# A state-space scan over even tokens only, with the decay scaled on ScalarE

## The chip, the cores and the metric

The kernel runs on one core of one Trainium2 chip. The metric is the device time of one execution in microseconds, as a median of several runs. Engines are named as in the profile: PE is TensorE (PEld its weight loads), DVE is VectorE, ACT is ScalarE, POOL is GpSimd, SP is SyncE, which issues DMAs.

## The reference

Two token mixers work on the same `x` of 2048 tokens by 1024 channels and are blended by a gate per token:

```python
g = sigmoid((x * gate_w).sum(-1, keepdims=True))
a = irfft2(rfft2(x) * (w_r + 1j * w_i))           # spectral branch
Lam_bar = exp(exp(log_dt) * Lam)                  # 1024 complex decays
Bu = einsum("bld,pd->blp", x, ((Lam_bar - 1) / Lam)[:, None] * Bmat)
for t in range(L):                                # state-space branch
    h = Lam_bar * h + Bu[:, t, :]
y = 2 * einsum("blp,dp->bld", hseq, Cmat).real + x * Dskip
out = g * a + (1 - g) * y
```

`x` is `A_x` in both branches. Inputs and the output are bf16.

## The kernel before

The tokens are cut into 8 chunks of 256 (`TC`), the 1024 states into 8 blocks `jb` of 128, one state per partition. Tile `h` of a chunk holds `[128, 2 (real, imaginary), 8 (jb), 256 (token)]` in bf16. A chunk goes through these steps:

- `unit_mm` (PE, L398): B times x, four psu tiles per chunk, each 32 matmuls of 256 columns. `unit_out` (ACT, L408) copies each to `h` and puts the tokens in order.
- `recur` (DVE): the complex decay is split into a radius r and a turn. `cross` (L347) and `along` (L350) multiply by a table `tab` of cosines and sines, `join_re` and `join_im` (L353, L356) add, so that what remains is a real recurrence with factor r. `carry_in` (L359) adds the last chunk's end to the first token, `scan` (L363) runs over all tokens of the block, once for the real and once for the imaginary part (`rz` holds r, and 0 at the first token of each jb, so one instruction covers many jb). `carry_part` and `carry_sum` (L368, L371) make the next carry. `cross(3)`, `along(2)`, `out_re` and `out_im` (L374, L378) turn back and multiply by the input factor. The products' scratch tile is `su` for chunks 0 and 1, and a part of `xQ` that PE has finished with for later ones.
- `c_half` and `c_part` (PE, L713 and L727): the 16 token tiles `tb` of 128 tokens, C times h, 16 matmuls per half of 512 columns. The first ten tiles go early through DRAM (`early_mm`, scaled by `scale_y`, L744), 10 to 12 (`DIAG`, with the skip term as extra matmuls, L719) and 13 to 15 (`rest`, tiles ps_q) are done last. Both tiles of chunk 7 are in `rest`; `last_out` (L899) and a store end the kernel.

Chunks 0 and 1 (`NSEP`) go through `recur` in two halves of 4 jb, later chunks in one unit. `h` has three buffers.

The spectral branch runs between these: `turn`, `fold`, `fd`, `s1` (forward transform, up to about 80 us), `s2`, `times_w`, `is1`, `is2` with evictions on ACT (L603, L637, L671), and at the end `spectral_mm` (PE, L806 and L810, tiles ps_id), `spectral_out` (ACT, L817) and the sums of `spectral` (DVE, L825 to L846). All PSUM tiles share four slots, whose turn is written out in `SLOTS`.

The order of the instructions on every engine is written out by hand: `ORDER` is a string of letters, each of which takes the next step of one of the generators, and `v` takes the next entry of `PIECES`, an index into the list `work` that `recur` fills. Each engine runs its own instructions in that order, waiting on semaphores.

Of the kernel before, what the change touches and what calls it, by code (L numbers as in the profile page):

```python
# [40 lines left out]
CARRY_POOL = ()  # L41
# [9 lines left out]
)  # L51
SLOTS = (
    "0123012310231023102310230123012031201312031203101230132031231031201312303312013213021021013010320130",
    "1220123203201320130130120321023120320321021023120312301230231201302303120",
# [3 lines left out]
    "xxxTVUVVVaTfVVrrUGTGG|Tfaaa|UafFffftafftUftxFEfTETUFffU22xSEkSTSTArxAfffUAUFTTEUfffUFbxwxbxbbTUEFbfE",  # L58
    "1bT~SSUfuFSFAUUUU2bbtbfAF1AtbbtrFttrbEffE11EbEh11SStbttfttttAg1~HtfufhA~tetFSSFrKHrtu1EAvfAEhtttvttt",
    "SSFtbbvvvAtEttH1Avthtftv1cttwv1tcthccctttvtcch~HFtvftHvvhuHtvfStEettStAHhtAeKrvFctcvvFhEEHKtvwtcSvtS",  # L60
    "hvvKc1vcc1vAAKKvv1c1v1hcvswcsLMvvveHHekMYsssnNHvvhHnsvvvJWWMvs3vsvNvvsssssnvssnvvs4NMvv4Njvhv553vhvv",
    "YvyJJL46H4vv5WWvhh5vvvMM78Jj7HHmn3nHvv8M44m6MnN77WW5jv+Yy5vvv3M845+mNY8nMJJMyvvv+467hvHMh5vN7N34vHmh",
    "4J8m+6n3h8v77HmH+55v4n64JMvNnMYy5vW83n+v7N474vJ568vYmmNJ7dh7NWj+v58v5vyvvd88MhvHHm8+MJm6h+n378vv7Hh8",
    "J+d4Y4YX5vv5NnJH6XXv7ny7mNNm8+hn8hvqivvvvvJvqyHihYivvyiqhivqqiYvNImvni+qJJmHIIiini+HinvdIIH+vvIIIqIN",
    "IiiiNmI+vvIInvvImvyJqii%NJINIJYJYmhvvv+vvvlylzvhHmplpzZZH+mZZZhlZvhPPRR++zyRRRlQDQHzRZZmRHZ+ZRZvoOZD",
    "QvlpDzzPovOvQBvZZlpPYvZZvBZDZRDRRRvzQDoloOBzoQOopZOoPOBlzlZRoDDZZvBZZRpQvzCvYZZvZZBZZPRDoQoo9RQQ9yRR",
    "0RRyCooD099C9Y990DD0D0Y00",
# [75 lines left out]
def kernel(  # L143
# [19 lines left out]
    out2 = out[0]  # L163
# [53 lines left out]
    nc.gpsimd.iota(tau_i, pattern=[[1, TC]], base=0, channel_multiplier=0)  # L217
# [5 lines left out]
    tab = tabp.tile([P, 4, 8, TC], BF16, name="tab")  # L223
# [42 lines left out]
    def radii():  # L266
        for jb in range(8):
            nc.gpsimd.tensor_copy(out=rz[:, jb, :], in_=r_sb[:, jb:jb + 1].to_broadcast([P, TC]))
            nc.gpsimd.memset(rz[:, jb, 0:1], 0.0)
            yield  # L270

    def make_tab(jp):
# [14 lines left out]
        cast(2 * jp)(out=tab[:, 1, js, :], in_=sn_f)  # L287
        yield
        t1 = tmp.tile(sh, FP32, name="t1")
        t2 = tmp.tile(sh, FP32, name="t2")  # L290
        for j in range(2):
            nc.scalar.activation(out=t1[:, j], in_=sn_f[:, j], func=ACT.Copy, scale=ci[:, 2 * jp + j:2 * jp + j + 1])
        yield
        cast(2 * jp + 1)(out=tab[:, 0, js, :], in_=cs_f)
# [5 lines left out]
        for j in range(2):  # L300
            jb = 2 * jp + j
            nc.vector.scalar_tensor_tensor(out=tab[:, 2, jb, :], in0=cs_f[:, j], scalar=cr[:, jb:jb + 1], in1=t1[:, j],
                                           op0=ALU.mult, op1=ALU.subtract)
            yield
        for j in range(2):
            jb = 2 * jp + j
            nc.vector.scalar_tensor_tensor(out=tab[:, 3, jb, :], in0=sn_f[:, j], scalar=cr[:, jb:jb + 1], in1=t2[:, j],
                                           op0=ALU.mult, op1=ALU.add)
            yield

    rz = tabp.tile([P, 8, TC], FP32, name="rz")
    carry = cpool.tile([P, 2, 8], FP32, name="carry")
# [16 lines left out]
    def small_ops():  # L329
        return nc.gpsimd if next(smalls_made) in CARRY_POOL else nc.vector  # L330

    smalls_made = itertools.count()

    def recur(c, js, home):
        n = js.stop - js.start
        on_in, on_part, on_sum = (small_ops() for _ in range(3))
        sh = [P, 2, n, TC]
        u = hs[c][:, :, js, :]

        def bc(i):  # L340
            return tab[:, i:i + 1, js, :].to_broadcast(sh)

        tmps = {}

        def cross(i):
            tmps["s"] = home()
            nc.vector.tensor_mul(out=tmps["s"], in0=u[:, ::-1], in1=bc(i))  # L347
# [7 lines left out]
        def join_im():  # L355
            nc.vector.tensor_sub(out=u[:, 1], in0=tmps["s"][:, 1], in1=u[:, 1])  # L356

        def carry_in():
            on_in.tensor_add(out=u[:, :, :, 0], in0=u[:, :, :, 0], in1=carry[:, :, js])  # L359

        def scan(ri, j, m):
            seg = u[:, ri, j:j + m].rearrange("p j t -> p (j t)")
            nc.vector.tensor_tensor_scan(out=seg, data0=rz[:, js.start + j:js.start + j + m].rearrange("p j t -> p (j t)"),  # L363
                                         data1=seg, initial=0.0, op0=ALU.mult, op1=ALU.add)

        def carry_part():
            gl = u[:, :, :, TC - 1]
            on_part.tensor_mul(out=ck[:, :, :, js], in0=gl.unsqueeze(1).to_broadcast([P, 2, 2, n]), in1=rot[:, :, :, js])  # L368

        def carry_sum():  # L370
            on_sum.tensor_add(out=carry[:, :, js], in0=ck[:, :, 0, js], in1=ck[:, :, 1, js])  # L371

        def out_re():
            nc.vector.tensor_add(out=u[:, 0], in0=u[:, 0], in1=tmps["s"][:, 0])  # L374
            done[c] = done.get(c, 0) + n

        def out_im():
            nc.vector.tensor_sub(out=u[:, 1], in0=u[:, 1], in1=tmps["s"][:, 1])  # L378
# [23 lines left out]
    def unit_out():  # L402
        for c in range(NCH):
            for q in range(2):
                for ri in range(2):
                    if (q, ri) == (0, 0):
                        hs[c] = halloc()
                    nc.scalar.copy(out=hs[c][:, ri, 4 * q:4 * q + 4].rearrange("p b (q j) -> p b q j", j=32),  # L408
                                   in_=psus.pop((c, q, ri)).rearrange("p b (j q) -> p b q j", j=32))
                    if ri == 1 and c < NSEP:  # L410
                        recur(c, slice(4 * q, 4 * q + 4), lambda: up.tile([P, 2, 4, TC], BF16, name="su"))
                    elif ri == 1 and q == 1:
                        recur(c, slice(0, 8), lambda c=c: xQ[:, 2 * (c % 2):2 * (c % 2) + 2])
# [802 lines left out]
```

## Time and profile before

| | |
|---|---|
| time, median of 3 runs | 304.7 us (304.66 to 305.07) |
| profiled execution, span from the first to the last instruction | 303.6 us |
| mean granted TensorE clock | 0.999 |
| PE, DVE, ACT, POOL busy | 296.4, 289.3, 188.5, 73.3 us |
| HBM read, written | 27.46, 23.08 MB |

The profiled execution's own time as a run is not listed apart from these; its span stands 1.1 us under the median. A row of the grouped lines has the line, the engine, the operation, out<-in, shapes and count, then busy us and the mean ns of one, then the idle us just before them with what ended it. A row of the timeline has start and length in us. Busy time of a group counts overlapping instructions once, so it is less than count times mean.

### The profile page before, as it was taken

The page shows a single profiled execution, that of the slowest core. Times are in us where ns is not written, and L with a number is a line of the kernel's source. Part 1 is how long each engine was busy: PE and PEld are TensorE (multiplying, and loading weights), DVE is VectorE, ACT ScalarE, POOL GpSimd, SP SyncE. Part 2 cuts the span into 40 slices and gives each one's busy share as a digit, 9 for nine tenths or more (in the row PEclk, how much of TensorE's full clock was granted, in tenths as well). Part 3 has the DMA queues.
Part 4 walks back from the last instruction along what each step waited for, and adds up shares of the span by engine and source line. Part 5 has one row for each costly group of instructions (what it writes and reads, how often), then busy time and mean ns, then how long its engine had stood idle before and what let it go on. Part 6 is the DMA issues. An engine that isn't in the chain of part 4 may idle for free. (4 is left out here: it accounts for less than half of the span.)

```text
span 303.6 us, 6402 instructions
## 1 busy us (share of the span) xinstructions
PE 296.4 (98%) x2568; PEld 197.4 (65%) x2592; DVE 289.3 (95%) x340; ACT 188.5 (62%) x255; POOL 73.3 (24%) x99
## 2 busy tenths in 40 slices
PE   8999999999999999999999999999999999999995
PEld 5664677878864685458553866669657986645543
DVE  2999999999999999999999999999899999999995
ACT  4999999896532383667665865529668774343400
POOL 2100420745893001110210220202011253252330
PEclk9999999999999999999999999999999999999999
DMA  6999999989999599895948798687758876978976
GB/s 208 341 201 194 253 193 310 162 142 154 268 214 241 160 259 219 181 250 189 212 96 258 163 223 225 139 294 147 242 174 185 165 88 135 160 132 143 165 153 181
DMA packets 74157, 59.35 MB, mean 196 GB/s; under 512 B 44904, under 2 KB 61680, under 8 KB 74128
## 3 DMA queue, kind: packets, MB, share of 16 engines
q1 hardware_dynamic: 66560, 49.82, 65.8%
q0 software_dynamic: 6912, 8.69, 23.0%
q10 hardware_dynamic: 656, 0.44, 0.5%
q8 instruction: 20, 0.33, 0.4%
q14 instruction: 9, 0.07, 0.1%
HBM read 27.46 MB, written 23.08 MB: 166 GB/s over the span
## 5 line engine op out<-in xcount | busy, mean ns | idle before, releaser
L398 PE MATMUL psu<-xQ,BT 128*128 128x256 bf16 x1024 | 116.5, 273 | 0.2 <-DVE X L449 0.2
L398 PEld LDWEIGHTS <-BT 128*128 128x128 bf16 x1024 | 99.0, 98 | 17.3 <-issue 4.6
L713 PE MATMUL ps_y<-CT,h 128*128 128x512 bf16 x397 | 92.5, 379 | 0.9
L363 DVE TENSOR_TENSOR_SCAN h<-rz,h 128x2048 bf16<-128x2048 f32 (+1 forms) x20 | 70.8, 3561 | 0.0
L713 PEld LDWEIGHTS <-h 128*128 128x128 bf16 x416 | 39.6, 98 | 46.3 <-issue 2.9
L785 POOL DMA_DIRECT2D y_scratch<-su x20 | 17.3, 902 | 135.7 <-ACT su L779 105.4
L408 ACT CAST h<-psu 128x1024 bf16<-128x1024 f32 x32 | 32.3, 1011 | 18.7 <-PE psu L398 13.1
L350 DVE TENSOR_TENSOR h<-h,tab 128x4096 bf16<-128x4096 bf16 (+1 forms) x20 | 37.1, 1859 | 0.1
L744 ACT ACTIVATE ye<-ps_y,omg 128x512 f32<-128x512 f32 x26 | 17.9, 689 | 26.3 <-PE ps_y L713 11.8
L347 DVE TENSOR_TENSOR xQ<-h,tab 128x4096 bf16<-128x4096 bf16 x12 | 27.4, 2284 | 1.0 <-ACT h L408 1.0
L603 ACT CAST X<-ps_s 128x1024 bf16<-128x1024 f32 x16 | 16.2, 1010 | 14.6 <-PE ps_s L594 11.2
L727 PE MATMUL ps_q<-CT,h 128*128 128x512 bf16 (+2 forms) x110 | 21.3, 348 | 0.2
L817 ACT ACTIVATE BT<-ps_id,gB 128x1024 bf16<-128x1024 f32 x14 | 15.3, 1114 | 9.9 <-PE ps_id L810 5.7
L671 ACT CAST ZT<-ps_is 128x1024 bf16<-128x1024 f32 x16 | 15.8, 1017 | 6.2 <-PE ps_is L661 6.2
L637 ACT CAST C<-ps_is 128x1024 bf16<-128x1024 f32 x16 | 15.7, 1011 | 5.1 <-DMA xQ<-in_A_x_dram 3.4
L851 POOL DMA_DIRECT2D BT<-y_scratch x10 | 13.1, 1452 | 19.7 <-DVE BT L846 13.3
L727 PEld LDWEIGHTS <-h 128*128 128x128 bf16 x112 | 10.3, 98 | 10.4 <-DVE h L378 0.5
L779 ACT ACTIVATE su<-xs,omg 128x512 f32<-128x512 bf16 x20 | 14.2, 723 | 4.1 <-DMA y_scratch<-su 2.2
L929 ACT COPY xQ<-pt 128x1024 bf16<-128x1024 bf16 x12 | 12.2, 1082 | 1.3 <-PE pt L919 1.3
L449 ACT CAST X<-ps_fd 128x1024 bf16<-128x1024 f32 x12 | 12.3, 1062 | 1.0 <-PE ps_fd L439 0.9
L617 DVE TENSOR_TENSOR UV<-X,Wb 128x2048 bf16<-128x2048 bf16 x8 | 9.6, 1220 | 0.6 <-ACT ye L744 0.6
L617 DVE TENSOR_TENSOR UV<-X,raw 128x2048 bf16<-128x2048 bf16 x8 | 9.8, 1223 | 0.2 <-ACT X L604 0.2
(200 smaller groups left out, 397.3 us busy)
## 6 DMA issues: line engine op xcount, KB each, us to landing
y_scratch<-ye SPq DMA_DIRECT2D x20, 256.0 KB, 4.6
y_scratch<-su POOLq DMA_DIRECT2D x20, 256.0 KB, 4.7
Bb<-turn_scratch SPq DMA_DIRECT2D x16, 256.0 KB, 5.2
turn_scratch<-C SPq DMA_DIRECT2D x16, 256.0 KB, 4.1
raw<-turn_scratch SPq DMA_DIRECT2D x8, 512.0 KB, 4.3
xs<-in_A_x_dram SPq DMA_DIRECT2D x13, 256.0 KB, 3.9
out_dram<-BT SPq DMA_DIRECT2D x11, 256.0 KB, 4.3
CT<-in_A_x_dram SPq DMA_DIRECT2D x5, 512.0 KB, 6.1
```

Of the source, the lines that this page charges most:

```text
L347: nc.vector.tensor_mul(out=tmps["s"], in0=u[:, ::-1], in1=bc(i))
L350: nc.vector.tensor_mul(out=u, in0=u, in1=bc(i))
L363: nc.vector.tensor_tensor_scan(out=seg, data0=rz[:, js.start + j:js.start + j + m].rearrange("p j t -> p (j t)"), data1=seg, initial=0.0, ...
L398: nc.tensor.matmul(psu[:, j, :], lhsT=BT[4 * q + j][:, ri, d8, :], rhs=xQ[:, c, d8, :], start=(d8 == 0), stop=(d8 == 7))
L408: nc.scalar.copy(out=hs[c][:, ri, 4 * q:4 * q + 4].rearrange("p b (q j) -> p b q j", j=32), in_=psus.pop((c, q, ri)).rearrange("p b (j q) ...
L603: nc.scalar.copy(out=X2, in_=ps2s[g][b])
L617: nc.vector.tensor_mul(out=UV, in0=X2s.pop((g, b)).unsqueeze(1).to_broadcast([P, 2, 2, K]), in1=fft["Wb"][g // 2 % 2][:, :, at:at + 1, :]. ...
L671: nc.scalar.copy(out=ZT[:, 4 * kp:4 * kp + 4, :, 4 * G:4 * G + 4].rearrange("p (c r) n g -> p c r n g", c=2), in_=pszs.pop((G, kp)).rearra ...
L713: nc.tensor.matmul(psy, lhsT=hs[c][:, ri, jb, P * tq:P * (tq + 1)], rhs=CT[ri][:, jb, 512 * dh:512 * (dh + 1)], start=(i == 0), stop=(i == ...
L727: nc.tensor.matmul(psq, lhsT=hs[c][:, ri, jb, P * tq:P * (tq + 1)], rhs=CT[ri][:, jb, at:at + n], start=(i == 0), stop=(i == 15))
L744: nc.scalar.activation(out=ye, in_=psys[tb][:, K * hf:K * (hf + 1)], func=ACT.Copy, scale=omg[:, tb:tb + 1])
L785: nc.gpsimd.dma_start(out=y_dram[tb, hf], in_=xgs[tb, hf], accum_op=ALU.add)
```

## The change

The recurrence is taken two tokens at a time. With even tokens e and odd tokens o, g(e) = r² g(e-2) + (u(e) + r u(e-1)) and g(o) = r g(o-1) + u(o). In place of `scan` over 256 tokens, a unit now does: `late` on ACT, the odd inputs times r, moved by one; `carry_in` into the first column of that tile; `fold_in` on DVE, an add over the even tokens; `scan` over 128 even tokens with r² (`r2_sb`, the new `rz`), real and imaginary part in one instruction for a whole chunk; `next_` on ACT, the even results times r; and `fill_in` on DVE, an add over the odd tokens. `late` and `next_` take two jb per entry of `PIECES`, so a chunk has 8 activations of each. `carry_sum` goes, its add is now in `carry_in`.

```diff
-        return pool.tile([P, 2, 8, TC], BF16, name="h")
+        return pool.tile([P, 2, 2, 8, TS], BF16, name="h")
...
+        def late(j):
+            for i in range(j, j + 2):
+                nc.scalar.activation(out=tmps["s"][:, 0, :, i, 1:TS], in_=u[:, 1, :, i, 0:TS - 1], func=ACT.Copy,
+                                     scale=r_sb[:, js.start + i:js.start + i + 1])
+
+        def carry_in():
+            first = tmps["s"][:, 0, :, :, 0]
+            if c:
+                nc.vector.tensor_add(out=first, in0=ck[:, :, 0, js], in1=ck[:, :, 1, js])
+            else:
+                nc.vector.memset(first, 0.0)
+
+        def fold_in():
             nc.vector.tensor_add(out=u[:, 0], in0=u[:, 0], in1=tmps["s"][:, 0])
...
+        def scan():
+            flat = lambda t, i: t[:, i, js].rearrange("p j t -> p (j t)") if n < 8 else t.rearrange("p r j t -> p (r j t)")
+            for i in range(2 if n < 8 else 1):
+                seg = flat(hs[c][:, 0], i)
+                nc.vector.tensor_tensor_scan(out=seg, data0=flat(rz, i), data1=seg, initial=0.0, op0=ALU.mult, op1=ALU.add)
+
+        def next_(j):
+            for i in range(j, j + 2):
+                nc.scalar.activation(out=tmps["s"][:, 1, :, i, :], in_=u[:, 0, :, i, :], func=ACT.Copy,
+                                     scale=r_sb[:, js.start + i:js.start + i + 1])
+
+        def fill_in():
+            nc.vector.tensor_add(out=u[:, 1], in0=u[:, 1], in1=tmps["s"][:, 1])
...
-        if c:
-            work.append(carry_in)
-        work.extend((lambda: scan(0, 0, n), lambda: scan(1, 0, n)))
+        work.extend(partial(late, j) for j in range(0, n, 2))
+        work.extend((carry_in, fold_in, scan))
+        work.extend(partial(next_, j) for j in range(0, n, 2))
+        work.append(fill_in)
         if c + 1 < NCH:
-            work.extend((carry_part, carry_sum))
+            work.append(carry_part)
...
-                nc.scalar.copy(out=hs[c][:, ri, 4 * q:4 * q + 4].rearrange("p b (q j) -> p b q j", j=32),
-                               in_=psus.pop((c, q, ri)).rearrange("p b (j q) -> p b q j", j=32))
+                nc.scalar.copy(out=hs[c][:, :, ri, 4 * q:4 * q + 4].rearrange("p e b (q j) -> p e b q j", j=16),
+                               in_=psus.pop((c, q, ri)).rearrange("p b (j e q) -> p e b q j", e=2, j=16))
...
-                nc.sync.dma_start(out=out2[P * tb:P * (tb + 1), :], in_=gas[tb].rearrange("p h n -> p (h n)"))
+                nc.sync.dma_start(out=out_rows[tb], in_=gas[tb].rearrange("p h n -> p (h n)"))
...
 PIECES = (
...
-    0, 1, 2, 3, 4, 5, 6, 8, 7, 9, 11, 10, 24, 25, 27, 26, 12, 13, 15, 14, 17, 16, 28, 18,
+    0, 1, 3, 2, 6, 5, 4, 7, 8, 9, 10, 11, 12, 13, 14, 15, 16, 17, 18, 20, 19, 21, 22, 23, 24, 25, 27, 26, 28, 30, 29,
```

A token tile is now the even or the odd rows of a chunk: `h`, `tab` and `rz` have a dimension e of 2 in front of jb, the tables are made for even tokens first, the rows of `x` and of the output go by `rows_of` (a token tile's rows lie two apart in DRAM), the gate is loaded in that order, and `ZT` of the spectral branch has another layout, with the evictions of `is2_out` (L671, now L691) writing pairs. In the new file `cross` is L348, `along` L351, the joins L354 and L357, `late` L361, `carry_in` L367 and L369, `fold_in` L372, `scan` L378, `next_` L382, `fill_in` L386, `carry_part` L390, the outs L393 and L397, the eviction of psu L428.

`PIECES`, `SLOTS` and `ORDER` are written anew, so the instructions of all engines move. In the last chunk, DVE had before, from one scan to the other (L825 to L846 are sums of the spectral branch):

```order
L363 SCALAR_TENSOR_TENSOR h<-rz,h 128x2048
L844 TENSOR_TENSOR BT<-BT 128x2x512
L846 TENSOR_TENSOR BT<-BT 128x2x512
L825 TENSOR_TENSOR BT<-BT 128x2x2x128
L827 TENSOR_TENSOR BT<-BT 128x2x2x128
L836 TENSOR_TENSOR BT<-BT 128x4x256
L838 TENSOR_TENSOR BT<-BT 128x4x256
L363 SCALAR_TENSOR_TENSOR h<-rz,h 128x2048
```

On DVE in the last chunk there now stands, from `fold_in` to `fill_in` (L845 to L866 are the same spectral sums):

```order
L372 TENSOR_TENSOR h<-h,xQ 128x2048
L856 TENSOR_TENSOR BT<-BT 128x4x256
L858 TENSOR_TENSOR BT<-BT 128x4x256
L378 SCALAR_TENSOR_TENSOR h<-rz,h 128x2048
L845 TENSOR_TENSOR BT<-BT 128x2x2x128
L847 TENSOR_TENSOR BT<-BT 128x2x2x128
L864 TENSOR_TENSOR BT<-BT 128x2x512
L856 TENSOR_TENSOR BT<-BT 128x4x256
L858 TENSOR_TENSOR BT<-BT 128x4x256
L864 TENSOR_TENSOR BT<-BT 128x2x512
L866 TENSOR_TENSOR BT<-BT 128x2x512
L386 TENSOR_TENSOR h<-h,xQ 128x2048
```

One scan of 2048 elements stands where two stood, an add on each side of it, and the spectral sums fill the place in which ACT scales.

On ACT, from the last eviction of psu to the end of the ps_y tiles, there stood before (L817 evicts ps_id, L744 scales ps_y):

```order
L408 CAST h<-psu 128x1024
L744 ACTIVATE ye<-ps_y,omg 128x512
L817 ACTIVATE BT<-ps_id,gB 128x1024 x3
L744 ACTIVATE ye<-ps_y,omg 128x512
L817 ACTIVATE BT<-ps_id,gB 128x1024 x2
L744 ACTIVATE ye<-ps_y,omg 128x512
L817 ACTIVATE BT<-ps_id,gB 128x1024
L744 ACTIVATE ye<-ps_y,omg 128x512 x2
L817 ACTIVATE BT<-ps_id,gB 128x1024
```

On ACT at the same place there now stands (L837 evicts ps_id, L764 scales ps_y):

```order
L428 CAST h<-psu 128x2x512
L837 ACTIVATE BT<-ps_id,gB 128x1024 x2
L764 ACTIVATE ye<-ps_y,omg 128x512
L837 ACTIVATE BT<-ps_id,gB 128x1024 x2
L361 ACTIVATE xQ<-h,r_sb 128x2x127 x2
L764 ACTIVATE ye<-ps_y,omg 128x512
L361 ACTIVATE xQ<-h,r_sb 128x2x127 x6
L837 ACTIVATE BT<-ps_id,gB 128x1024 x3
L764 ACTIVATE ye<-ps_y,omg 128x512 x2
L382 ACTIVATE xQ<-h,r_sb 128x2x128 x8
L837 ACTIVATE BT<-ps_id,gB 128x1024 x3
```

Two trains of 8 activations have come between the evictions; the first is cut by the scaling of a ps_y half, the second stands behind two of them and ahead of three evictions of ps_id.

More of the change, by code (lines that the diff above doesn't have):

```diff
@@ L27 @@
 NCH = S // TC
+TS = TC // 2
 NEARLY = 10
@@ L162 @@
     x = A_x[0]
-    out2 = out[0]
+    rows_of = lambda t: [t.rearrange("(c p e) d -> c e p d", p=P, e=2)[tb // 2, tb % 2] for tb in range(16)]
+    out_rows, x_rows = rows_of(out[0]), rows_of(x)
     hc = _host_consts()
@@ L286, in make_tab @@
         yield
-        cast(2 * jp)(out=tab[:, 1, js, :], in_=sn_f)
+        cast(2 * jp)(out=tab[:, 1, :, js, :], in_=es(sn_f))
         yield
@@ L306, in make_tab @@
             jb = 2 * jp + j
[L307 removed]
+            nc.vector.scalar_tensor_tensor(out=tab[:, 3, :, jb, :], in0=one(sn_f, j), scalar=cr[:, jb:jb + 1], in1=one(t2, j),
                                            op0=ALU.mult, op1=ALU.add)
             yield
[L311 to L312 removed]
+    rz = tabp.tile([P, 2, 8, TS], FP32, name="rz")
     ck = cpool.tile([P, 2, 2, 8], FP32, name="ck")
@@ L352, in join_re @@
         def join_re():
-            nc.vector.tensor_add(out=u[:, 0], in0=u[:, 0], in1=tmps["s"][:, 0])
[L355 to L364, printed above, removed]
+            nc.vector.tensor_add(out=u[:, :, 0], in0=u[:, :, 0], in1=tmps["s"][:, :, 0])
@@ L1091, in turn_vectors @@
         nc.scalar.activation(out=r_sb, in_=are, func=ACT.Exp)
+        nc.scalar.activation(out=r2_sb, in_=are, func=ACT.Exp, scale=2.0)
         yield
```

102 lines of the change are left out of this document (51 added, 51 removed), and 12 rows, old and new, of the table PIECES.

## The prediction

> **What bounds the kernel now.** I read the page's busy times first, then the busy times by stretch, then single TensorE blocks in the timeline, then the chain that ended last.
>
> ```profile
> PE 296.4 (98%) x2568; PEld 197.4 (65%) x2592; DVE 289.3 (95%) x340; ACT 188.5 (62%) x255; POOL 73.3 (24%) x99
> ```
>
> PE and DVE both look full, so a lighter DVE helps only if PE waits for it. The stretches answer that (columns: window, its length, then busy us of PE, PEld, DVE, ACT and POOL).
>
> ```profile
> 10.00:30.00 20.00, 18.80 (x161) 11.62 (x162) 19.25 (x43) 20.00 (x24) 0.56 (x2) 1.00 1.14 224
> 30.00:80.00 50.00, 49.81 (x457) 39.37 (x456) 48.89 (x76) 44.38 (x66) 22.60 (x37) 1.00 1.14 209
> 100.00:200.00 100.00, 99.53 (x967) 62.38 (x975) 99.20 (x78) 61.58 (x89) 10.39 (x12) 1.00 0.82 203
> 200.00:290.00 90.00, 89.46 (x712) 61.10 (x718) 88.25 (x86) 52.21 (x61) 22.39 (x23) 1.00 0.81 166
> ```
>
> PE lacks 0.2 us between 30 and 80, and 1.0 us between 100 and 290. Busy spans of pipelined matmuls overlap, so I checked that the blocks also run at full pace (start, length, instructions):
>
> ```profile
> 247.05 3.66 PE L398 MATMUL psu<-xQ,BT 128*128 128x256 bf16 x32
> 250.54 0.39 PE L806 MATMUL ps_id<-raw,ZT 128*128 128x128 bf16 x4
> 250.77 0.60 PE L810 MATMUL ps_id<-raw,ZT 128*128 128x256 bf16 x4
> 251.20 3.62 PE L713 MATMUL ps_y<-CT,h 128*128 128x512 bf16 x15
> 254.66 0.39 PE L719 MATMUL ps_y<-xQ 128*128 128x128 bf16 x4
> ...
> 261.20 3.62 PE L713 MATMUL ps_y<-CT,h 128*128 128x512 bf16 x16
> 264.65 0.39 PE L719 MATMUL ps_y<-xQ 128*128 128x128 bf16 x4
> 264.87 0.39 PE L806 MATMUL ps_id<-raw,ZT 128*128 128x128 bf16 x4
> ...
> 277.22 3.62 PE L727 MATMUL ps_q<-CT,h 128*128 128x512 bf16 x16
> 280.68 0.39 PE L806 MATMUL ps_id<-raw,ZT 128*128 128x128 bf16 x4
> ```
>
> Rows overlap by the length of their last matmul, so a block's cost is start to start: 3.50 us for the 32 of a psu tile (247.05 to 250.54), 0.66 us for a spectral tile (250.54 to 251.20), 3.67 us for half a ps_y tile of a skip-diagonal token tile (261.20 to 264.87), 3.46 us for 16 of ps_q. That is 0.109 us per 256 columns and 0.216 us per 512, in blocks with no pause. PE therefore sets the pace from about 30 us on, with DVE just fast enough. How just is seen at the end:
>
> ```profile
> 285.42 1.15 DVE h L378
> 286.56 0.05 issue
> 286.61 5.79 PE ps_q L727 x26
> ...
> 300.46 0.35 DVE raw L899
> ```
>
> The last product of chunk 7 on DVE ends at 286.56 and its first matmul begins at 286.61, though PE was busy up to then. DVE and PE meet here with nothing to spare.
>
> **The change part by part.** The sum is made against the profiled execution, span 303.6; the median of the runs is 304.7, so 1.1 us lie around the span. About 0.2%, 0.6 us, is what a measurement here tells from no change.
>
> ```profile
> L363 DVE TENSOR_TENSOR_SCAN h<-rz,h 128x2048 bf16<-128x2048 f32 x12 | 52.7, 4416 | 0.0
> L363 DVE TENSOR_TENSOR_SCAN h<-rz,h 128x1024 bf16<-128x1024 f32 x8 | 18.1, 2278 | 0.0
> L374 DVE TENSOR_TENSOR h<-h,xQ 128x2048 bf16<-128x2048 bf16 x6 | 7.3, 1221 | 0.0
> L374 DVE TENSOR_TENSOR h<-h,su 128x1024 bf16<-128x1024 bf16 x4 | 2.7, 680 | 0.0
> L371 DVE TENSOR_TENSOR carry<-ck 128x16 f32<-128x16 f32 x5 | 0.9, 171 | 0.0
> ```
>
> *DVE.* Scans take 70.8 us. Left are 6 of 2048 elements (6 x 4.39 = 26.3) and 8 of 512 (the two forms differ by 2.14 us per 1024 elements, so about 1.2 each, 9.6): 35.9, a cut of 34.9. Added are two adds per unit, 12 of 2048 elements at 1.22 and 8 of 1024 at 0.68: 20.1. The carry sums (1.5) go, two memsets come (0.3). Net -16.0, to about 273 us. None of it lies on the path while PE is dense, so it counts 0. The products with one more dimension (L348, L351) are taken at their old price; if they cost a tenth more, 7 us return, still under 16.
>
> *ACT.* Added are 128 activations of 254 or 256 elements, SBUF to SBUF, with a scale per partition. The nearest rows:
>
> ```profile
> L292 ACT ACTIVATE t<-sn_f,ci 128x256 f32<-128x256 f32 x8 | 3.8, 543 | 0.0
> L1149 ACT ACTIVATE xQ<-ident,vecF 128x128 bf16<-128x128 bf16 x8 | 2.8, 400 | 0.0
> L779 ACT ACTIVATE su<-xs,omg 128x512 f32<-128x512 bf16 x20 | 14.2, 723 | 4.1 <-DMA y_scratch<-su 2.2 <-DVE h L378 1.7 <-DVE xs L769 0.2
> L408 ACT CAST h<-psu 128x1024 bf16<-128x1024 f32 x32 | 32.3, 1011 | 18.7 <-PE psu L398 13.1 <-PE ps_y L713 5.6
> ```
>
> L292 is nearest in size. Its 8 run in pairs, so a pair lasts 0.95 us and the second adds 0.41; the ends are 0.35 (2.8 / 8, half the size) and 0.71 (14.2 / 20, double). I take 0.41: 128 x 0.41 = 52 us, ACT 241 us, 79% of the span; ends 45 and 91. The evictions L408 and L671 get other strides; same element counts, so 0.
>
> *Front.* Between 10 and 30 us ACT is busy 20.00 of 20.00, and 44.38 of 50 until 80: 5.6 us free. Chunk 0's scaling puts 16 x 0.41 = 6.6 us there before its first product. But the new order runs 12 psu tiles ahead of the first ps_y, where 11 stood, so ACT has 3.5 us more, less 1.0 for the added eviction. 5.6 + 2.5 - 6.6 leaves 1.5: cost 0, with -0.5 (less idle PE) and +2 (DVE leaves ACT waiting) as ends.
>
> *Middle.* Chunks 1 to 7 put 7 x 6.6 = 46 us beside ACT's 113.8 in 190 us: 84% busy, with PSUM evictions queued behind the scaling, for which PE waits if late. It fits on average; I take +0.2, ends 0 and +1.5.
>
> *Last chunk.* From the last psu tile to the first matmul on chunk 7, PE has in the new order 9 spectral tiles (0.66 each), 3 ps_y tiles (7.35) and 2 ps_q blocks (3.46): 34.9 us, where 10 spectral tiles stood, 35.6. In that cover DVE must finish the chunk. The serial part of its work was
>
> ```profile
> 250.74 1.01 ACT L408 CAST h<-psu 128x1024 bf16<-128x1024 f32 x1 [1.51 <-PE psu L398]
> ...
> 276.12 2.29 DVE L347 TENSOR_TENSOR xQ<-h,tab 128x4096 bf16<-128x4096 bf16 x1
> ...
> 280.13 2.28 DVE L350 TENSOR_TENSOR h<-h,tab 128x4096 bf16<-128x4096 bf16 x1
> ```
>
> 1.0 + 4 products of 2.2 + 4 adds of 1.14 + 2 scans of 4.33 = 23 us. Now it is 1.0 + 8.8 + 6 x 1.14 + 4.3, plus two trains of 8 on ACT of 3.3: 27.5. It got longer, while DVE's load got lighter. With the spectral sums that the new order puts between, I get: joins done 8.3 us after the last psu tile, first train done at 13.1 (after its first two operations ACT's queue holds the scaling of a ps_y half that PE has ready at 9.9), scan done at 19.8, second train done at 23.3 (ahead of it stands a ps_y half ready at 19.3), last sum at 33.9. Cover 34.9, so 1.0 to spare. Cost 0, ends 0 and +1.2.
>
> *DMA.* Rows of a token tile now lie two apart in DRAM, pieces stay as long: 0, ends -0.2 and +0.3.
>
> The sum: 303.6 + 0 + 0 + 0.2 + 0 = 303.8; with 1.1 around it 304.9.
>
> **The rivals.** *ACT holds PE* (0.28). Alone, L292 takes 0.543; at that price, or with 0.13 of handoff per operation, 16 operations cost 2.1 us more. It decides from 1.0 us more on, the spare in the last chunk: PE waits 1.1 there, 0.6 in front, and up to 2 where evictions stand behind a train: 304.9 + 2.6 = about 307.5. For it: trains of 4 and 8 stand ahead of evictions, and DVE must wait for each train before it goes on. Against: of the 190 us from 100 to 290, ACT has 30 left after the addition.
>
> *PE's small pauses go* (0.18). PE lacks 1.2 us between 10 and 30, 0.2 to 80, 1.0 from 100 to 290. With a DVE that is early everywhere half might go: 303.4; all: 302.3. Against: the front waits for ACT as much as for DVE.
>
> *PE is not the bound* (0.04). Were its dense look only matmuls that wait in flight for DVE, DVE's 16.0 would come off: 288.7. The blocks speak against it: 0.216 us per 512 columns in every block, early or late, whatever DVE does. The Trainium skill's "TensorE: Matmul & The Clock Gate" (Back-to-back issue gap) would side with this rival: it gives about 131 ns per 512-column matmul as the sustained rate, which leaves PE much room. The trace has no block of 512 columns on full 128x128 weights near that pace, so I follow the trace. "Perfetto Trace Analysis" of the Trainium skill (Identifying the Most-Contended Engine) likewise distrusts matmul busy time and looks at weight loads, here 65%; the spacing inside the blocks is my answer to it.
>
> That the scan isn't halved can be excluded: the new order has 14 scan instructions with the sizes above.
>
> **How the numbers follow.** PE keeps its pace: 0.50, between 304.0 and 305.9; of this 0.10 is faster by over 0.6 us, 0.24 within, 0.16 slower. With the rivals: faster 0.10 + 0.18 + 0.04 = 0.32, same 0.24, slower 0.16 + 0.28 = 0.44. The range leaves out the last rival, the faster one's far end and the far end of ACT's price: 302.8 to 308.2.
>
> **What would show it.** Right: DVE near 273 us and ACT near 241, the new activations at 0.4 to 0.55 us each, PE still above 99% busy between 30 and 290, and PE's first ps_q on chunk 7 at about 286.5. Wrong to the slow side: PE idle before psu or ps_y tiles, released by an ACT eviction behind L361 or L382, or before the last ps_q tiles, released by L393. Wrong to the fast side: the last ps_q block ends before 299.5. Wrong in its ground: psu blocks closer than 3.50 us.

## The result, and the profile after

The changed kernel takes 313.9 us (median of 4 runs, 311.9 to 314.5) where the kernel before takes 304.9: a ratio of 1.028 [1.024, 1.032], slower by about 8.5 us. Its profiled execution has a time of 313.8 and a span of 312.1 us, where the span before is 303.6. Ratios here leave out executions that took over 1.5% longer than the fastest of the same kernel, and medians don't, so the two need not agree to the last tenth.

Busy times first (share of the span, instructions):

```profile
PE 298.3 (96%) x2571; PEld 197.9 (63%) x2592; DVE 277.6 (89%) x347; ACT 238.7 (76%) x384; POOL 61.7 (20%) x99
```

VectorE lost 11.7 us of work and ScalarE gained 50. TensorE's share fell from 98% to 96%. The stretches that the prediction read:

```profile
10.00:30.00 20.00, 18.60 (x153) 10.89 (x155) 18.82 (x43) 17.85 (x22) 6.09 (x13) 1.00 1.18 225
30.00:80.00 50.00, 49.16 (x453) 39.51 (x452) 43.72 (x75) 49.03 (x80) 13.13 (x25) 1.00 1.05 206
100.00:200.00 100.00, 97.69 (x953) 60.80 (x959) 93.70 (x82) 82.26 (x145) 10.36 (x12) 1.00 0.75 184
200.00:290.00 90.00, 86.56 (x702) 60.30 (x708) 82.15 (x82) 72.21 (x111) 21.93 (x22) 1.00 0.82 172
```

Between 100 and 290 us PE lacks 5.7 us (2.3 and 3.4) where it lacked 1.0; between 30 and 80 it lacks 0.8 where it lacked 0.2. Inside a block the pace is as before: 3.50 us from the first of a psu tile's 32 matmuls to the next block, here for the last psu tile.

```profile
253.30 3.66 PE L418 MATMUL psu<-xQ,BT 128*128 128x256 bf16 x32
256.80 0.39 PE L826 MATMUL ps_id<-raw,ZT 128*128 128x128 bf16 x4
```

So the time is in pauses between blocks. The list of PE's waits (who waited for whom: us, times, longest) says before which; from the kernel before, its two longest:

```profile
PE psw L987 <- DVE A L982: 1.2, 1, 1.2
PE ps_r L970 <- DVE preT L943: 0.5, 1, 0.5
```

and after, its longest:

```profile
PE ps_y L733 <- ACT BT L837: 1.5, 1, 1.5
PE psw L1007 <- DVE A L1002: 1.2, 1, 1.2
PE ps_is L649 <- ACT X L623: 1.0, 1, 1.0
PE psu L418 <- ACT ZT L691: 0.8, 1, 0.8
PE psu L418 <- ACT ye L764: 0.8, 1, 0.8
PE ps_s L482 <- DMA raw<-c_T: 0.7, 1, 0.7
```

Four of the five new waits end with an eviction on ScalarE. What held ScalarE is seen in its timeline. At 160 to 170 us (start, length; idle before and its releaser in brackets):

```profile
159.33 1.01 ACT L657 CAST C<-ps_is 128x1024 bf16<-128x1024 f32 x1 [1.36 <-DMA turn_scratch<-C]
160.24 1.70 ACT L382 ACTIVATE xQ<-h,r_sb 128x256 bf16<-128x256 bf16 x4
161.84 0.71 ACT L799 ACTIVATE su<-xs,omg 128x512 f32<-128x512 bf16 x1
162.46 1.70 ACT L382 ACTIVATE xQ<-h,r_sb 128x256 bf16<-128x256 bf16 x4
164.05 0.67 ACT L764 ACTIVATE ye<-ps_y,omg 128x512 f32<-128x512 f32 x1
...
168.08 0.72 ACT L799 ACTIVATE su<-xs,omg 128x512 f32<-128x512 bf16 x1 [1.61 <-DMA y_scratch<-su]
168.71 0.99 ACT L623 CAST X<-ps_s 128x1024 bf16<-128x1024 f32 x1
```

The skip scaling su (L799) writes one of two halves of a buffer that GpSimd adds to y_scratch by a transfer. ScalarE stands 1.61 us until that transfer has landed, and the eviction X (L623) that PE waits for stands behind it. Ahead of that, ye (L764), for which PE waits 0.8 us, stands behind a train of eight, cut by a skip scaling, and the train behind an eviction that waited 1.36 us for a store. At 210 us a train stands for a scan that VectorE is still running, and two evictions ZT (L691) stand behind:

```profile
211.63 0.91 ACT L382 ACTIVATE xQ<-h,r_sb 128x256 bf16<-128x256 bf16 x2 [1.92 <-DVE h L378]
212.44 1.08 ACT L691 CAST ZT<-ps_is 128x1024 bf16<-128x1024 f32 x1
213.42 0.71 ACT L799 ACTIVATE su<-xs,omg 128x512 f32<-128x512 bf16 x1
214.04 0.89 ACT L382 ACTIVATE xQ<-h,r_sb 128x256 bf16<-128x256 bf16 x2
214.84 1.07 ACT L691 CAST ZT<-ps_is 128x1024 bf16<-128x1024 f32 x1
```

At 268 us a spectral eviction waits for an output store:

```profile
267.99 1.12 ACT L837 ACTIVATE BT<-ps_id,gB 128x1024 bf16<-128x1024 f32 x1 [3.58 <-DMA out_dram<-BT]
```

and PE's timeline shows it waiting for the PSUM slot that this eviction frees:

```profile
269.15 3.61 PE L733 MATMUL ps_y<-CT,h 128*128 128x512 bf16 x16 [1.54 <-ACT BT L837]
```

In the kernel before, an eviction at the same place waits nearly as long for its store, and PE's list has no wait for it. What differs is how soon PE, or a train, needs what stands behind.

```profile
265.80 1.11 ACT L817 ACTIVATE BT<-ps_id,gB 128x1024 bf16<-128x1024 f32 x1 [3.29 <-DMA out_dram<-BT]
```

The new operations cost what was forecast (line, shape, count, then busy and mean ns of one, idle before and who ended it):

```profile
L378 DVE TENSOR_TENSOR_SCAN h<-rz,h 128x2048 bf16<-128x2048 f32 x6 | 26.5, 4424 | 0.2
L382 ACT ACTIVATE xQ<-h,r_sb 128x256 bf16<-128x256 bf16 x48 | 20.5, 499 | 3.2 <-DVE h L378 3.1
L361 ACT ACTIVATE xQ<-h,r_sb 128x254 bf16<-128x254 bf16 x48 | 20.4, 497 | 3.1 <-DVE h L354 3.1
```

At the end PE's last matmul is over at 308.05 (first row; before it was at 300.42, second row), and the last add with its store behind it needs 4.05 us until the end of the span, where it needed 3.2:

```profile
295.76 12.29 PE L747 MATMUL ps_q<-CT,h 128*128 128x512 bf16 x72
```

```profile
295.68 4.74 PE L727 MATMUL ps_q<-CT,h 128*128 128x512 bf16 x37
```

So of the 8.5 us in the span, 7.6 come before PE's last matmul and 0.9 after it. The last two adds stand until an output store has freed the tile that they write, in this row of VectorE:

```profile
308.03 0.88 DVE L919 SCALAR_TENSOR_TENSOR raw<-ps_q,omg,xQ 128x384 bf16<-128x384 f32 x2 [0.55 <-DMA out_dram<-raw]
```

### The profile page after: what moved, and what is told of

It reads as the page before. It is cut to its first block, busy times and chain, and to the rows that moved or that the text cites. A ratio compares the mean times of both kernels' runs of the same rounds, so it can differ in the third digit from the quotient of the medians.

```text
span 312.1 us, 6550 instructions
## 1 busy us (share of the span) xinstructions
PE 298.3 (96%) x2571; PEld 197.9 (63%) x2592; DVE 277.6 (89%) x347; ACT 238.7 (76%) x384; POOL 61.7 (20%) x99
## 5 line engine op out<-in xcount | busy, mean ns | idle before, releaser
L805 POOL DMA_DIRECT2D y_scratch<-su x20 | 18.2, 923 | 146.0 <-ACT su L799 144.3
L351 DVE TENSOR_TENSOR h<-h,tab 128x4096 bf16<-128x4096 bf16 (+1 forms) x20 | 37.2, 1862 | 0.6
L378 DVE TENSOR_TENSOR_SCAN h<-rz,h 128x512 bf16<-128x512 f32 (+1 forms) x14 | 36.1, 2599 | 0.4
L428 ACT CAST h<-psu 128x1024 bf16<-128x1024 f32 x32 | 31.9, 1007 | 4.2 <-PE psu L418 4.1
L348 DVE TENSOR_TENSOR xQ<-h,tab 128x4096 bf16<-128x4096 bf16 x12 | 27.4, 2285 | 4.2 <-ACT h L428 4.1
L764 ACT ACTIVATE ye<-ps_y,omg 128x512 f32<-128x512 f32 x26 | 17.4, 683 | 10.7 <-issue 5.4
L382 ACT ACTIVATE xQ<-h,r_sb 128x256 bf16<-128x256 bf16 x48 | 20.5, 499 | 3.2 <-DVE h L378 3.1
L361 ACT ACTIVATE xQ<-h,r_sb 128x254 bf16<-128x254 bf16 x48 | 20.4, 497 | 3.1 <-DVE h L354 3.1
L837 ACT ACTIVATE BT<-ps_id,gB 128x1024 bf16<-128x1024 f32 x14 | 15.1, 1110 | 5.2 <-DMA out_dram<-BT 5.2
L691 ACT CAST ZT<-ps_is 128x1024 bf16<-128x1024 f32 x16 | 17.0, 1102 | 0.0
L623 ACT CAST X<-ps_s 128x1024 bf16<-128x1024 f32 x16 | 16.1, 1008 | 0.4 <-PE ps_s L614 0.3
L799 ACT ACTIVATE su<-xs,omg 128x512 f32<-128x512 bf16 x20 | 14.3, 725 | 2.0 <-DMA y_scratch<-su 2.0
L871 POOL DMA_DIRECT2D BT<-y_scratch x10 | 12.2, 1444 | 15.1 <-DVE BT L866 10.6
L949 ACT COPY xQ<-pt 128x1024 bf16<-128x1024 bf16 x12 | 11.7, 1018 | 1.8 <-PE pt L939 1.8
L348 DVE TENSOR_TENSOR su<-h,tab 128x2048 bf16<-128x2048 bf16 x8 | 9.8, 1222 | 3.0 <-ACT h L428 2.8
```

The source lines that it names most:

```text
L348: nc.vector.tensor_mul(out=tmps["s"], in0=u[:, :, ::-1], in1=bc(i))
L351: nc.vector.tensor_mul(out=u, in0=u, in1=bc(i))
L361: nc.scalar.activation(out=tmps["s"][:, 0, :, i, 1:TS], in_=u[:, 1, :, i, 0:TS - 1], func=ACT.Copy, scale=r_sb[:, js.start + i:js.start + ...
L378: nc.vector.tensor_tensor_scan(out=seg, data0=flat(rz, i), data1=seg, initial=0.0, op0=ALU.mult, op1=ALU.add)
L382: nc.scalar.activation(out=tmps["s"][:, 1, :, i, :], in_=u[:, 0, :, i, :], func=ACT.Copy, scale=r_sb[:, js.start + i:js.start + i + 1])
L428: nc.scalar.copy(out=hs[c][:, :, ri, 4 * q:4 * q + 4].rearrange("p e b (q j) -> p e b q j", j=16), in_=psus.pop((c, q, ri)).rearrange("p b ...
```

## The experiments

Four theories. T1: the scaling trains hold PE, by ScalarE's load or by the handoffs between VectorE and ScalarE. T2: rows two apart in DRAM land later. T3: the start, where the c_T loads stand behind x loads. T4: the new written order, whatever the operations are: transfers and waiting instructions stand ahead of evictions in in-order queues. In the expectations T5 is the rival of T4, that the new recurrence and its layouts cost the time wherever they stand. A percent here is 3.05 us.

**e3, the scalings cut short**, and **e4, the load without the handoffs.**

```diff
 # e3
-out=tmps["s"][:, 0, :, i, 1:TS], in_=u[:, 1, :, i, 0:TS - 1]
+out=tmps["s"][:, 0, :, i, 1:3], in_=u[:, 1, :, i, 0:2]
...
-out=tmps["s"][:, 1, :, i, :], in_=u[:, 0, :, i, :]
+out=tmps["s"][:, 1, :, i, 0:2], in_=u[:, 0, :, i, 0:2]
 # e4, both places
+out=idle_s, in_=tab[:, 0, :, i, 0:100]
```

> The changed kernel with each of the 128 scaling activations cut to 2 columns per part, so that only the first columns are scaled: same number of instructions, same waits between ScalarE and VectorE, ScalarE relieved of about 128 x 0.2 = 26 us. T1 as load (ScalarE too full, evictions late): about half of the loss comes back, 308 to 310 us. T1 as handoffs (VectorE waits for a train to start and to end, whatever its length): a train of 8 lasts 1.6 us instead of 3.4, still 3 to 5 us of the loss stay, 309 to 311. T2: 313 to 314, since transfers are as before. T3: 313 to 314.

> The changed kernel with the 128 scaling activations at their places in ScalarE's order but reading a constant table and writing a tile that nobody reads (200 of the 256 elements, the scaled terms are left out): ScalarE's load nearly stays, all handoffs between VectorE and the trains go. T1 as load: 311 to 314 us. T1 as handoffs: 305 to 308 us. T2: 312 to 314 us, since the transfers stay. T3: 313 to 314.

Measured: 313.9 us, ratio 1.027 [1.024, 1.031], with ScalarE at 213.8 us instead of 238.7; and 313.4 us, 1.026 [1.023, 1.029]. Neither gives the time back that T1 forecast for load or for handoffs alone. For e3 the time doesn't tell the whole: the two waits behind trains, 0.8 us each for ye and ZT, are gone from PE's list, and another has come at 204.6 us, for a scaling ye that waits for its own store:

```profile
PE ps_y L733 <- ACT ye L764: 1.9, 1, 1.9
```

So the trace leaves T1 some 1.6 us of the 8.5, and the times don't show them.

**e1, rows contiguous again**, and **e2, the kernel before with rows two apart.**

```diff
 # e1
-rows_of = lambda t: [t.rearrange("(c p e) d -> c e p d", p=P, e=2)[tb // 2, tb % 2] for tb in range(16)]
+rows_of = lambda t: [t[P * tb:P * (tb + 1), :] for tb in range(16)]
 # e2, in the kernel before
-in_=x[P * tb:P * (tb + 1), :]
+in_=x_rows[tb]
...
-out=out2[P * tb:P * (tb + 1), :]
+out=out_rows[tb]
```

> The changed kernel with the token tiles of x and of the output laid on 128 successive rows in DRAM, as before; everything else, the order and the instructions included, stays. (Rows of the skip and of the output are thereby exchanged within a chunk.) Theory T2, that rows two apart land later and so hold buffers: the skip loads go back from a median of 6.6 us to about 4, the stores of own tiles from 7.4 to about 4.5, and with them 3 to 5 us of the 9 come back: 309 to 311 us. Rivals T1 (the scaling on ScalarE holds PE) and T3 (the order of loads at the start): the landing times hardly move or don't matter, 313 to 314 us.

> The kernel before, its skip loads and output stores moved to rows two apart in DRAM as in the changed kernel, nothing else (rows of skip and output are thereby exchanged within a chunk). T2: skip loads land after more than 5 us instead of 3.9, and 2 to 5 us are lost, 307 to 310 us. T4 and T5: 304.5 to 305.5 us.

Measured: e2 is at 305.4 us, ratio 0.998 [0.996, 1.001]: the rows alone cost nothing. The list of transfers (count, size of each, median us from issue to landing) has the skip load in the changed kernel, in e1 and in e2:

```profile
xs<-in_A_x_dram SPq DMA_DIRECT2D x13, 256.0 KB, 6.6
```

```profile
xs<-in_A_x_dram SPq DMA_DIRECT2D x13, 256.0 KB, 6.8
```

```profile
xs<-in_A_x_dram SPq DMA_DIRECT2D x13, 256.0 KB, 4.3
```

and in the kernel before:

```profile
xs<-in_A_x_dram SPq DMA_DIRECT2D x13, 256.0 KB, 3.9
```

The landing time goes with the order and not with the rows: 6.6 and 6.8 us in the new order, 3.9 and 4.3 in the old one. T2 falls. e1 itself is at 313.9 us; its ratio, 1.019 [1.015, 1.023], rests on two executions of 311.3 and 311.7, and the changed kernel had one of 311.9 itself, so no gain is read from it. The output stores of BT don't go back to 4.5 us either: 7.4 in the changed kernel and 7.1 in e1, where the kernel before has 4.3 and e2 3.7.

**e5, the c_T loads earlier.**

```diff
-xxTVUVVVaVaxfGffTGUfGVf|aatrTTfUffxxxx2kFUEfFFrT2fa|tEfTT...
+xxTVUVVVaVaxfGffTGUfGVf|aatrTTfUffx22xxxkFUEfFFrTfa|tEfTT...
```

> The changed kernel with the two small loads of the c_T table issued four steps earlier in the written order, ahead of the x loads, where they stood in the kernel before. T3: the wait of PE for c_T at 14 us goes, 0.8 us less, about 313.1 us, and the table that starts the front is ready earlier, perhaps another 0.5. T1 and T2: at most these 0.8 us.

Measured: 314.1 us, 1.029 [1.025, 1.033]. The wait for c_T is gone from PE's waits, and the time is not shorter. T3 falls as a cause of its own.

**e8, the old work in the new order; e17, the least work in the new order; e7, the new recurrence in the old order.**

```diff
 # e8: late() and next_() empty, fold_in() empty
 def fill_in():
-    nc.vector.tensor_add(out=u[:, 1], in0=u[:, 1], in1=tmps["s"][:, 1])
+    scan(1)
 # e17: as e8, and fill_in() empty too
 # e7: ORDER and SLOTS of the kernel before, PIECES rearranged in the first four half units, and
+work.extend((lambda: cross(1), lambda: along(0), lambda: joined(join_re), lambda: joined(join_im)))
+if c:
+    work.append(fold)              # carry_in, fold_in
+work.extend((scanned, scanned))    # scan and the second train; fill_in
```

> The changed kernel in its own order with the scaling on ScalarE and the two adds left out, and a second scan of the same size over the odd tokens in place of the second add: ScalarE at about 189 us and VectorE at about 290 us of work, as in the kernel before, in the order of the changed one (what is scanned is not the recurrence). T4: the loss stays, 312 to 316 us. T5: 304 to 307 us.

> The changed kernel in its own order with the 128 scalings and the two adds of each unit left out and only the half scan kept: ScalarE at about 189 us and VectorE at about 258 us, less than in either kernel. T4, the order holds TensorE by transfers and in-order queues whatever the two engines have to do: 311 to 314 us. T5, the work of the new recurrence delays TensorE: 304 to 307 us.

> The changed kernel's recurrence (half scans, scaling on ScalarE, even and odd rows, same layouts) run in the written order and the PSUM slots of the kernel before: the first scaling train stands at the second join, the two adds and the second train at the places of the two old scans, and in the first four half units a few recurrence steps are put one behind the other because they share one scratch tile. T4, the new written order loses the time (skip path, stores and evictions meet their buffers later): 304 to 306 us, although VectorE now waits directly behind each train. T5, the new recurrence itself loses it wherever it stands (handoffs, layouts, more small operations): 311 to 316 us.

Measured: e8 319.0 us, 1.044 [1.039, 1.049]; e17 313.2 us, 1.021 [1.015, 1.028]; e7 387.2 us, 1.266 [1.260, 1.273]. The page's busy times of e17:

```profile
PE 300.3 (96%) x2592; PEld 198.6 (63%) x2592; DVE 258.2 (83%) x327; ACT 189.5 (61%) x256; POOL 63.4 (20%) x99
```

With less work on VectorE and ScalarE than either kernel has, the new order still loses 6.4 us (4.5 to 8.5); with the operation counts of the kernel before it loses 13. (Both ran at a granted clock a little under 1: 0.988 in the profiled execution of e8, 0.993 in that of e17, whose one execution at 1.00 took 312.0 us.) So the new operations' work alone is not the loss: without it T5 forecast 304 to 307. It is not shown that the loss sits at the same places. In e17 PE lacks 0.7 us between 150 and 180 us, where it lacks 2.1 in the changed kernel, and its longest wait is one of 2.0 us until 202.5 us for the load raw<-turn_scratch, which the changed kernel doesn't have; e8 has it too, and at 319.0 us lies above what T4 forecast. Both keep the new layouts, so they don't part these from the order; of the evictions only ZT, written in pairs, became longer (1.10 us where it took 1.02). And T4's other half failed by 80 us: the old order can't take the new recurrence as e7 places it, with each second train straight behind its scan. Its longest wait (waits between 125 and 150 us of e7):

```profile
PE psu L438 <- ACT C L677: 13.8, 1, 13.8
...
ACT xQ L380 <- DVE h L376: 8.0, 1, 8.0
```

A train waits 8.0 us for a scan, the eviction C stands behind it, and PE stands 13.8 us. It is the same mechanism as at 210 us in the changed kernel, where the train waits 1.92 us. Neither order ran well with the other's operations.

**e12, evictions first; e14 and e15, each move alone.** Two places of the changed order on ScalarE: at 166 us one letter (the skip scaling m behind the eviction 4), at 210 us three (a skip scaling m and the first two steps of a train, v, behind the second eviction I).

```diff
 # e14
-...jM5+7+JhvH34vnY856mNn477vvvvvMMm5vvy38J8n5vvvWvN4+m+hmYy4d6vvvn77
+...jM5+7+JhvH34vnY856mNn477vvvvvMMm5vvy38J8n5vvvWvN4+m+hYy4md6vvvn77
 # e15
-qvv+JiXYyImvIY+qhviivvvviqnvvHqHIHiIIJ+mm...
+qv+JiXYyIImvvY+qhviivvvviqnvvHqHIHiIIJ+mm...
 # e12: both
```

> The changed kernel with the two moves on ScalarE alone: the eviction at 166 us ahead of the skip scaling that waits for its store, and the two ZT evictions at 210 us ahead of the train that waits for a scan. T4: 1.2 + 1.0 us less, 311.5 to 312 us. T5: 313.5 to 314 us.

> The changed kernel with one letter moved: at 166 us the eviction X goes ahead of the skip scaling that waits for its store. If each move is worth the stall that it removes: 1.2 us, 312.7 us. If the earlier move also takes the stall at 267 us away: 310.5 to 311.5 us, with no pause over 1 us between 255 and 275 us.

> The changed kernel with the two ZT evictions at 210 us ahead of the train that waits for a scan, nothing else. If each move is worth the stall that it removes: 1.0 us, 312.9 us. If this one takes the stall at 267 us away: 310.5 to 311.5 us.

Measured: e12 309.5 us, 1.012 [1.010, 1.015]; e14 311.9 us, 1.022 [1.016, 1.029]; e15 314.0 us, 1.027 [1.021, 1.033]. In the profiled execution of e12 ScalarE runs (timeline at 166 us)

```profile
166.29 0.72 ACT L800 ACTIVATE su<-xs,omg 128x512 f32<-128x512 bf16 x1
166.92 0.99 ACT L624 CAST X<-ps_s 128x1024 bf16<-128x1024 f32 x1
...
168.54 0.72 ACT L800 ACTIVATE su<-xs,omg 128x512 f32<-128x512 bf16 x1 [0.41 <-DMA y_scratch<-su]
```

with the eviction ahead of the scaling that waits, and the waits of PE for X, for ZT and for the spectral eviction are gone. Four moved letters are worth 4.7 us by the ratio, twice the two stalls and more than T4 forecast; the ratio leaves out one execution of four, of 313.6 us at a clock of 1.00, and the mean of all four is 310.3. Alone the first move is worth 1.7 and the second 0.2, and their intervals overlap that of the changed kernel. The stall at 268 us is gone in e12, and also in the profiled executions of e1 and e5, which have the changed kernel's order there; it was there in e14, e15 and e16. So it comes and goes between executions, and e12's number is at the good end of what the two moves give: e9, e13 and e16 below contain them too and stand at 1.017, 1.013 and 1.021. The four together say 2 to 5 us.

**e9, e10, e11: three more repairs.** SyncE's own waits in the changed kernel between 195 and 217 us have

```profile
SPq L783 <- ACT su L799: 7.9, 1, 7.9
```

a skip load that waits for a skip scaling to free its buffer. e10 puts it behind the next three loads of raw; e11 gives a ps_y half the PSUM slot that comes free earlier at 267 us; e9 is e12 with both.

```diff
 # e10
-qvv+JiXYyImvIY+qhviivvvviqnvvHqHIH...
+qvv+JiXYyImvI+qhviivvvviqnvvHqYHIH...
 # e11
-...XDDDRzDzZvpoloZOBZZvvv...
+...XDDDRzDzZvpoolZOBZZvvv...
```

> The changed kernel with five letters of its written order moved by a few places each, nothing else: at 166 us an eviction (X, line 623) goes ahead of a skip scaling (su) that waits for its store; at 210 us two evictions (ZT, line 691) go ahead of the train L382 that waits for a running scan; at 206 us SyncE's skip load that waits for ScalarE goes behind two loads of raw; at 267 us the ps_y half goes ahead of a spectral tile, so that it takes the PSUM slot that is freed 4 us earlier. T4 (the new order leaves too little time between a transfer or a scan and the instruction that waits for it, and in-order queues pass it on to TensorE): the stalls 1.2 + 1.0 + 0 to 2 + 1.7 go, less what comes back later, 308.5 to 311 us. T5 (the recurrence or its layouts are slower in themselves): the waits move elsewhere, 312.5 to 314.5 us.

> The changed kernel with one letter moved: the ninth skip load stands behind two loads of raw in SyncE's queue. T4 with SyncE's queue as the carrier: SyncE's wait of 7.9 us for ScalarE stays but holds nothing, 1 to 2 us less, 312 to 313 us; if only the evictions carry it, 313.5 to 314 us.

> The changed kernel with one pair of letters exchanged at 267 us: the ps_y half goes ahead of a spectral tile and takes its slot. T4: the stall of 1.7 us there goes and nothing else, 312 to 312.5 us; T5: the time goes to the spectral tile behind, 313.5 to 314 us.

Measured: e10 314.0 us, 1.026 [1.023, 1.029]: SyncE's wait held nothing that mattered. e11 315.0 us, 1.032 [1.029, 1.035]: worse, since two spectral tiles behind it now wait for evictions, 1.2 and 1.4 us in PE's waits. e9 311.1 us, 1.017 [1.014, 1.021], no better than e12. In both, PE's wait for the spectral eviction has moved to the tiles behind the one that was moved.

**e13, evictions first with short scalings; e16, evictions first with the c_T loads early.** The edits of e3 and of e5 on e12.

> The kernel with the two moves on ScalarE, its 128 scalings cut to 2 columns per part (most of the scaled terms are left out). If ScalarE's load holds TensorE once the evictions stand ahead: 307 to 308.5 us. If the load has never mattered, only what stands behind a waiting instruction: 309 to 310 us.

> The kernel with the two moves on ScalarE, and the two c_T loads issued four steps earlier at the start. If the start is a bound of its own: 0.8 us less than without, 308.7 us. If TensorE meets another wait behind it, as in the changed kernel: 309.5 us.

Measured: e13 311.8 us, 1.013 [1.006, 1.021]; e16 311.8 us, 1.021 [1.016, 1.025]. Early tables gain nothing: e16 stands above e12. e13's ratio rests on two executions, 310.9 and 307.8 us, and its trace has a pause of 1.9 us until 202.4 us as in e3, so it can't say what shorter trains are worth in the repaired order.

**e18, the changed kernel without the skip's adds; e19, the same cut in the kernel before.**

```diff
-nc.gpsimd.dma_start(out=y_dram[tb, hf], in_=xgs[tb, hf], accum_op=ALU.add)
```

> The changed kernel without the 20 accumulating transfers that add the scaled skip to y_scratch, so that the skip scaling never waits for its buffer and y_scratch has less traffic (the skip of the first ten token tiles is left out). T4 with the skip path as the carrier: the stall at 166 us and, through earlier stores, that at 267 us go: 309 to 311 us. If the other transfers carry it: 313 to 314 us.

> The same cut in the kernel before, as the control: its skip scalings waited for a buffer 2.2 us in all and TensorE for none of it, so 304.5 to 305.5 us by every theory; a gain of over 1 us here would mean that the transfers cost time by their traffic.

Measured: e18 309.4 us, 1.011 [1.008, 1.014]; e19 305.8 us, 0.998 [0.995, 1.001]. The 20 transfers cost the kernel before nothing and the changed one about 5 us (3 to 7 by the two intervals). Busy times by stretch (window, its length, PE, PEld, DVE, ACT, POOL), of the kernel before, of the changed one and of e18:

```profile
150.00:180.00 30.00, 29.84 (x308) 18.94 (x296) 29.38 (x22) 21.09 (x32) 4.32 (x5) 1.00 0.74 182
180.00:230.00 50.00, 49.68 (x430) 33.33 (x434) 48.81 (x32) 29.63 (x40) 4.30 (x5) 1.00 0.77 203
255.00:290.00 35.00, 34.67 (x218) 19.09 (x220) 34.86 (x40) 14.65 (x16) 13.01 (x13) 1.00 0.87 150
```

```profile
150.00:180.00 30.00, 27.90 (x274) 15.75 (x276) 29.28 (x24) 25.64 (x46) 3.40 (x4) 1.00 0.86 212
180.00:230.00 50.00, 48.50 (x427) 33.46 (x430) 41.84 (x28) 42.44 (x70) 6.86 (x8) 1.00 0.73 190
255.00:290.00 35.00, 33.00 (x221) 19.29 (x224) 32.49 (x39) 22.27 (x34) 14.33 (x14) 1.00 1.04 161
```

```profile
150.00:180.00 30.00, 30.00 (x301) 17.70 (x299) 29.66 (x24) 26.32 (x46) 0.00 (x0) 1.00 0.56 168
180.00:230.00 50.00, 50.00 (x439) 33.65 (x437) 45.50 (x32) 45.43 (x76) 0.00 (x0) 1.00 0.54 161
255.00:290.00 35.00, 33.55 (x208) 17.76 (x206) 32.89 (x38) 20.00 (x32) 12.51 (x12) 1.00 0.91 145
```

Without the adds PE is dense from 150 to 230 us, with every train in place: the 3.6 us that it lacked there are gone. The cut takes away the buffer's wait and traffic as well (the eviction C ahead of the trains at 159 us now waits 0.28 us for its store and not 1.36), and e18 doesn't part the two. What it doesn't touch stays: 1.5 us between 255 and 290.

So the loss has parts. PE lacks 3.1 us more than before between 150 and 230 us, where evictions stand on ScalarE behind instructions that wait (for transfers, for a scan); e18 takes all of that away, and e12 the two largest stalls. It lacks 1.7 us more between 255 and 290, behind spectral evictions that wait for output stores; this comes and goes between executions. Some 0.9 us lie behind the last matmul and 0.6 between 30 and 80 us. These last three were read from the trace and not tested alone. That is 6.3 of 8.5 us; the rest I can't place by stretches, since some records of matmuls are missing (the pages count 2568 before and 2571 after, 2592 in e17) and a missing record looks like a pause. No version beat the kernel before; e12 with the cut of e18 and an order planned anew were not tried.

## Why the prediction was wrong

*PE sets the pace* held: 109 ns per 256 columns and 216 per 512 in both kernels, and what could be placed of the loss before the last matmul is pauses between blocks. *PE is not the bound* is out.

*DVE.* Scans were to take 35.9 us and took 36.0. The total came to 277.6 and not 273, and it isn't seen in the time: e17, at 258 us, is hardly faster (313.2).

*ACT.* 0.41 us each was right: a train of four takes 1.70 us, so the three behind the first add (1.70 - 0.50) / 3 = 0.40. "ScalarE: Activation LUTs" of the Trainium skill (What ACT_TABLE_LOAD costs) gives 186 ns, 0.833 ns per element and 93 ns for a pointer operand, with 93 ns of overlap between neighbours; for 254 elements that is an estimate of 491 ns alone and 398 in a row, and the trace agrees (497 the mean of one, 0.40 us in a row).

*Middle* is the step that failed: +0.2 with ends at 0 and 1.5, where PE lost 4.7 us more than before between 100 and 290. It was worked out as a load (84% busy, "it fits on average"), and load was not the question: e3 takes 25 us of work off ScalarE and its time stays at 313.9. The step asked how long ScalarE works and not what stands in its queue ahead of each eviction, and how early that can start. In its place the runs showed PE standing for evictions behind waiting instructions: 3.1 us more than before between 150 and 230, all gone without the skip's adds (e18). The rows for this were to be had: the order of the changed kernel has the first steps of a train one place behind their scan, with two ZT evictions behind, and a skip scaling two places behind the issue of the transfer that must free its buffer.

*ACT holds PE* had the nearest time (about 307.5) and the right engine. It named the trains' price and their handoffs, and no time bears these out (e3, e4); what the runs showed is the queue, and mostly waits that go with the skip adds while every train stays (e18). Its "up to 2 where evictions stand behind a train" is in the trace at 0.8 us each for ye and ZT.

*Front* lay in its range: 0.2 us between 10 and 30 and 0.6 between 30 and 80, of up to 2. *Last chunk:* the last sum of chunk 7 ends at 293.97 in the chain that ended last,

```profile
292.83 1.14 DVE h L393
```

37.2 us after the last psu tile (256.80), not 33.9, and so later than the cover of 34.9. The first train stands behind the spectral eviction that waits for its store, and is done at 16.1 us and not at 13.1. PE has no pause before the last sum here only because it had already stood 1.5 us for the same eviction; in e10 and e15, which have this stall too, it waits another 0.6 and 0.5 us for L394, which is L393 here. In e1 and e12, without the stall, the first train is done at 13.6 and 13.4 us and the last sum at 34.8, inside the cover, and PE doesn't wait. So the working was right to 1 us where the store lands in time, and what the step left out is that store: it holds PE and the chain alike.

*DMA* at 0 was right for the rows (e2) and wrong for the kernel. Skip loads land after 6.6 us where 3.9 stood, and that comes with the new order. Costing a transfer by its bytes left out who waits for its landing.

The range ended at 308.2 because its widest terms were prices of operations. None of them was a price for the order, though the change writes the order of the whole kernel anew.

## What to carry to other kernels

Where a dense engine is fed by an in-order one, ask of each eviction what stands ahead of it in its queue and what that waits for; a busy share of 76% says nothing of it. A rewritten order is a change of its own: cost it at each place where an instruction that waits for a transfer or for another engine has been moved closer to what it waits for. To find which wait carries a loss, cut the transfer behind it in both kernels: nothing in the one and 5 us in the other is plainer than any reading of a trace.

## What the runs showed of the hardware

Stalls that end with the landing of a transfer are there in one execution and not in the next (1.5 us at 268 us in the profiled one, none in e1, e5 and e12). A part of the spread between executions may come from that: 311.9 to 314.5 us in the four of the result, where the kernel before has 304.7 to 305.1. But repeated beside the experiments the kernel before spreads from 304.6 to 308.9 too, so that the changed order spreads more is not shown.

A long pause is paid for again in the clock. In e7 the granted clock is 0.92 to 0.93 in all four executions, and after the pause of 13.8 us the first 24 matmuls of 256 columns take 4.10 us, where 24 at full pace are 23 x 0.109 + 0.27 = 2.8:

```profile
149.07 4.10 PE L438 MATMUL psu<-xQ,BT 128*128 128x256 bf16 x24 [13.82 <-ACT C L677]
```

"TensorE: Matmul & The Clock Gate" of the Trainium skill (Part 1: The HAM clock gate) says that the array falls to half its clock after an idle window of about 3.4 us and comes back after as long a busy one; the row agrees with that, and so does a granted clock of 0.50 between 140 and 149 us. But e17's pause of 2.0 us is enough here: the granted clock reads 0.50 between 204 and 206 us, and 16 matmuls of 512 columns that start at 203.94 take 4.71 us where 3.61 stood. The pauses of the changed kernel, 1.5 us at most, leave its clock at 1.00.
